# Transposing token tiles and attention outputs by DMA instead of on TensorE

## The chip, the cores and the metric

The kernel runs on one core of one Trainium2 chip. The metric is the device time of one execution in microseconds (us). A result is the median of the timed runs, with the lowest and highest in brackets.

Engines are named as in the profile: PE is TensorE, PEld its weight loads, DVE is VectorE, ACT is ScalarE, SP is SyncE, whose queue issues nearly all DMAs (SPq). Tiles lie in SBUF, the on-chip memory; the results of matmuls go to PSUM, a second one, which is divided into banks.

## The reference

Two layers are run twice with the same weights on 2048 tokens of width 1024 (x + A(norm x), then x + B(norm x)). A is a dilated local attention with 32 heads, window 8 and step 2: token s sees tokens s, s-2, ..., s-14. B is an MLP over the token axis: its first matmul sums over the tokens.

```python
def _A_ref(x, wqkv, wo):
    H = 32; Dh = D // H
    W, dil = 8, 2
    qkv = ((x @ wqkv).reshape(B, S, 3, H, Dh)).transpose(2, 0, 3, 1, 4)
    q, k, v = qkv[0], qkv[1], qkv[2]
    # ... gather of 8 keys and values a token, softmax over them ...
    o = jnp.einsum("bhsw,bhswd->bhsd", attn, vg)
    return o.transpose(0, 2, 1, 3).reshape(B, S, D) @ wo

def _B_ref(x, w1, b1, w2, b2):          # S = 2048, F = 3584
    h = _layernorm(x, axis=-1)
    u = _gelu(jnp.einsum("bsd,sf->bdf", h, w1) + b1)
    y = jnp.einsum("bdf,fs->bds", u, w2) + b2
    return y.transpose(0, 2, 1)

x = A_x
x = x + _A_ref(_layernorm(x), A_wqkv, A_wo)
x = x + _B_ref(_layernorm(x), B_w1, B_b1, B_w2, B_b2)
x = x + _A_ref(_layernorm(x), A_wqkv, A_wo)
x = x + _B_ref(_layernorm(x), B_w1, B_b1, B_w2, B_b2)
```

## The kernel before

Even and odd tokens never meet in attention, so they are two classes of 1024 tokens. A class is worked in four chunks of 8 heads: eight chunks a layer, four of class 0, then four of class 1. In a chunk TensorE makes q, k and v, and VectorE does scores, softmax and the weighted sum.

The kernel's matmuls sum over the partitions, the leading axis of a tile, so two things are transposed on TensorE: the normed tokens, before the q, k, v projections (`hT`), and the attention outputs, before the output projection (`oT`). A transpose on TensorE is a matmul against an identity. It leaves its result in PSUM, and ScalarE (in one case VectorE) copies it to SBUF.

```python
    stat = pool("stat", 4)
    x2p = pool("x2p", 5)
    hxp = pool("hxp", 4)
    pers = pool("pers", 1)
    wqp = pool("wqp", 2)
    wbp = pool("wbp", 6)
    otp = pool("otp", NQ)
    dram = pool("dram", 1, space=bass.MemoryType.DRAM)
    psmm = pool("psmm", 2, space=bass.MemoryType.PSUM)
    pstp = pool("pstp", 1, space=bass.MemoryType.PSUM)
    psop = pool("psop", 2, space=bass.MemoryType.PSUM)
    psgp = pool("psgp", 2, space=bass.MemoryType.PSUM)
# ... cut ...
    def ps_fill(k):
        pl, tag = ((psop, "pso"), (psgp, "psg"))[k % 2]
        return pl.tile([P, 512], FP32, name=tag, tag=tag)
# ... cut ...
    o_q = pers.tile([P, J, QW], BF16, name="o_q")
# ... cut ...
    g = [pers.tile([P, GF, D], BF16, name=f"g{n}") for n in range(NFB)]
# ... cut ...
    def transposes(h, tag="tpf"):
        tp = pstp.tile([P, KD, P], BF16, name="tp", tag=tag)
        for kt in range(KD):
            nc.tensor.transpose(tp[:, kt, :], h[:, kt * P:(kt + 1) * P], ident[:])
        return tp
# ... cut ...
    def prologue_tile(c, j, hT):
        t = g[(c * J + j) // GF][:, (c * J + j) % GF, :]
        if c:
            nm, rs = stats_act(t, 1.0, eps1)
            norm_act(t, t, nm, rs)
        else:
            mean, rs = stats_dve(t, 1.0, eps1)
            norm_dve(t, t, mean, rs)
        tp = transposes(t, "tpf" if c or j % 2 else "tpa")
        nc.scalar.copy(out=hT[c][j // JH][:, :, j % JH, :], in_=tp[:])
```

The kernel uses eight banks of PSUM: two for `ps`, one for each of the two tags of `pstp` (the transposes), two for `pso` and two for `psg`.

```python
                tf = T4[:].rearrange("p u j c -> p u (j c)")
                for n in range(W // WB):
                    self.weighted(ci, n * WB, WB, T4[:])
                    if n == 0:
                        nc.vector.tensor_tensor(out=of, in0=tf[:, 0], in1=tf[:, 1], op=ALU.add)
                        yield 0.0, 3.5
                    else:
                        nc.vector.tensor_tensor(out=tf[:, 0], in0=tf[:, 0], in1=tf[:, 1], op=ALU.add)
                        nc.vector.tensor_tensor(out=of, in0=of, in1=tf[:, 0], op=ALU.add)
                        yield 0.0, 4.8
            oT = otp.tile([P, 2, J, P], BF16, name="oT", tag="oT")
            self.oT[c][qi] = oT
            for b in range(2):
                tp = pstp.tile([P, J, P], BF16, name="tpo", tag="tpa")
                for j in range(J):
                    nc.tensor.transpose(tp[:, j, :], o_q[:, j, b * P:(b + 1) * P], ident[:])
                nc.scalar.copy(out=oT[:, b, :, :], in_=tp[:])
            yield 1.2, 0.0
```

There is one `o_q` buffer. The next chunk may write it only when the transposes of this chunk have read it.

```python
        for n in range(NDC):
            for hf in range(2):
                wt = wb("wo", [P, KD // 2, 512])
                for k in range(KD // 2):
                    kt = hf * (KD // 2) + k
                    nc.sync.dma_start(out=wt[:, k, :], in_=wo_v[kt // 2, kt % 2][:, :, n * 512:(n + 1) * 512])
                wo_t[n][hf] = wt
# ... cut ...
        for j in range(J):
            xr = x2("xr")
            nc.sync.dma_start(out=xr[:], in_=res_v[:, j, :])
            xn = x2("xn")
            s1 = st("s1", [P, NDC]) if on_act else None
            for n in range(NDC):
                ps = psop.tile([P, 512], FP32, name="pso", tag="pso")
                xs_ = slice(n * 512, (n + 1) * 512)
                for kt in range(KD):
                    nc.tensor.matmul(ps[:], lhsT=at_.oT[c][kt // 2][:, kt % 2, j, :], rhs=wo_t[n][kt // 4][:, kt % 4, :],
# ... cut ...
    def gemm1(h2, fb, classes, first, last):
        wt = {c: w1_tile(c, fb) for c in classes}
        nk = len(classes) * J
        for fl in range(GF):
            ft = fb * GF + fl
            for dc in range(NDC):
                ps = ps_both(fl * NDC + dc) if last and first else ps_fill(fl * NDC + dc)
                k = 0
                for c in classes:
                    for j in range(J):
                        nc.tensor.matmul(ps[:], lhsT=wt[c][:, j, fl * P:(fl + 1) * P],
                                         rhs=h2[c][j // JH][:, j % JH, dc * 512:(dc + 1) * 512],
# ... cut ...
    def gemm2_tile(c, i, w2t, src, dst, hT, on_act=False):
        xs = x2("xs")
        nc.sync.dma_start(out=xs[:], in_=src[c][i * P:(i + 1) * P, :])
        xo = x2("xo")
        for dc in range(NDC):
            ps = ps_fill(dc)
            for ft in range(FT):
                nc.tensor.matmul(ps[:], lhsT=w2t[ft // HF][:, ft % HF, c::DIL],
                                 rhs=g[ft // GF][:, ft % GF, dc * 512:(dc + 1) * 512],
                                 start=(ft == 0), stop=(ft == FT - 1))
# ... cut ...
            norm_dve(hb[:], xo[:], mean, rs)
        tp = transposes(hb)
        for jh in range(2):
            src_v = tp[:].rearrange("d kt (a jh j) -> d jh kt j a", jh=2, j=JH)[:, jh]
            dst_v = hT[c][jh][:, :, :, 16 * i:16 * i + 16]
            if on_act or jh == 0:
                nc.scalar.copy(out=dst_v, in_=src_v)
            else:
                nc.vector.tensor_copy(out=dst_v, in_=src_v)
        yield 0.6, 0.0 if on_act else 2.0
```

The sum of class 0's tokens over ten of the fourteen 256-wide blocks of F (320 matmuls, the "partials") needs only class 0's attention. It is issued as filling while VectorE is still busy with class 1. How far ahead it is issued is set by `weave`: each `yield` hands it a pair of numbers, an estimate in us of TensorE's and of VectorE's work, and it puts filling in while TensorE's sum is below VectorE's. Each block has one `w1` tile and four groups of eight matmuls, two in each pool.

```python
def partials():
    for fb in range(NPART):                      # NPART = 10
        yield from gemm1(h2, fb, (0,), True, False)

weave(at_.stream(), second_class(),
      chain(out_proj(at_, 0, res[0], xa[li][0], h2, on_act=True), partials()),   # filling
      out_proj(at_, 1, res[1], xa[li][1], h2, on_act=False))
for fb in range(NPART, NFB):
    run(gemm1(h2, fb, (0, 1), True, True))       # the other four blocks, both classes
for fb in range(NPART):
    run(gemm1(h2, fb, (1,), False, True))        # class 1's half of the ten
```

## Time and profile before

The median before is 1398.31 us (1396.37 to 1399.87, 4 runs). The profiled execution spans 1394.9 us at a granted TensorE clock of 0.983. These lines of the page say how busy the engines are in all, with the number of instructions at the end:

```profile
PE 1314.1 (94%) x7840; PEld 749.7 (54%) x7840; DVE 818.0 (59%) x928; ACT 483.4 (35%) x940; POOL 10.5 (1%) x20
```

94% is an average over stages with different limits, so the same is read by stretches. The table of busy time by stretch has, per row: start and end of the stretch, its length, then busy time and count for PE, PEld, DVE, ACT and POOL, then the granted clock (1.00 is full), the DMA share and GB/s. The stretches are the prologue, attention 1, the MLP of layer 1, the two halves of attention 2 (class 0 with the other class's second MLP matmul as filling; class 1), and the rest.

```profile
0.00:39.00 39.00, 24.02 (x208) 19.23 (x209) 15.74 (x36) 28.78 (x68) 10.49 (x20) 0.98 0.95 246
39.00:359.00 320.00, 300.01 (x2168) 203.85 (x2167) 295.45 (x300) 165.09 (x332) 0.00 (x0) 0.99 0.33 97
359.00:620.00 261.00, 259.73 (x1249) 118.66 (x1248) 88.52 (x144) 57.07 (x100) 0.00 (x0) 0.99 0.44 130
620.00:840.00 220.00, 207.48 (x1482) 140.06 (x1481) 175.32 (x174) 92.34 (x180) 0.00 (x0) 0.98 0.48 140
840.00:1034.00 194.00, 167.77 (x1107) 107.28 (x1104) 164.49 (x156) 90.91 (x182) 0.00 (x0) 0.95 0.34 97
1034.00:1395.00 361.00, 355.09 (x1636) 160.65 (x1636) 78.46 (x121) 49.26 (x79) 0.00 (x0) 0.99 0.34 101
```

Attention 1 belongs to VectorE (295 of 320 us), the two MLP stretches to TensorE (259.7 of 261, 355.1 of 361 us), and attention 2 is mixed. Since the last stretch is dense TensorE work, any matmul that can be done before 1034 us shortens it. That is what the filling is for.

Here is the end of attention 2, from the timeline of PE. A row has start, length, engine, source line, operation, output and inputs, count and, in brackets, idle time before it and what ended it. L466 is `gemm1`, L433 the output projection, L357 the transposes of the attention output.

```profile
1006.13 1.03 PE L466 MATMUL psg<-h_8331,w_9361 128*128 128x512 bf16 x4
1006.99 2.75 PE L433 MATMUL pso<-wo,oT 128*128 128x512 bf16 x12
1009.58 1.03 PE L466 MATMUL psg<-h_8330,w_9721 128*128 128x512 bf16 x4
...
1015.62 1.03 PE L466 MATMUL psg<-h_8331,w_9763 128*128 128x512 bf16 x4
1034.35 1.03 PE L357 MATMUL tpo<-ident,o_q 128*128 128x128 bf16 x8 [17.70 <-DVE o_q L350]
...
1039.99 10.36 PE L433 MATMUL pso<-wo,oT 128*128 128x512 bf16 x37 [0.36 <-DVE xn L439]
```

At 1006.99 us twelve matmuls of the output projection for class 1 start: two accumulations, six of the eight terms of each. Both `pso` banks are taken, and they can't be finished before the last chunk's `oT` exists, which has the other two terms. Then four groups run, all in `psg`, and TensorE stands for 17.70 us until VectorE has made the last `o_q`. The same stretch in the table of windows:

```profile
1016.00:1034.00 18.00, 0.65 (x4) 0.10 (x1) 17.55 (x12) 0.58 (x1) 0.00 (x0) 0.63 0.00 0
1034.00:1045.00 11.00, 8.95 (x33) 3.88 (x34) 4.38 (x9) 2.52 (x4) 0.00 (x0) 0.52 0.16 49
```

TensorE is busy 0.65 of 18 us, its granted clock is 0.63 and then 0.52, and no DMA moves (0 GB/s).

The longest wait of VectorE on the transposes is this line of the list of waits (who waited for what: us in total, times, longest), and the timeline around its end:

```profile
DVE o_q L346 <- PE tpo L357: 23.8, 1, 23.8
```
```profile
940.30 0.99 ACT L358 COPY oT<-tpo 128x1024 bf16<-128x1024 bf16 x1
...
941.34 0.61 PE L357 MATMUL tpo<-ident,o_q 128*128 128x128 bf16 x8
...
941.99 1.22 DVE L346 TENSOR_TENSOR o_q<-T_126 128x2048 bf16<-128x2048 bf16 x1 [23.78 <-PE tpo L357]
```

VectorE wants to write the next `o_q`, and the second half of the previous chunk's transposes has not read the old one. It waits for the copy at 940.30, which comes late in ScalarE's queue behind the norms of the output projection.

In the second MLP matmul, TensorE's timeline shows what one token tile's eight transposes cost:

```profile
604.99 0.38 PE L488 MATMUL pso<-g_138,w_5535 128*128 128x512 bf16 x1
605.52 0.62 PE L228 MATMUL tp<-ident,hb 128*128 128x128 bf16 x8 [0.16 <-DVE hb L218]
605.98 0.38 PE L488 MATMUL pso<-g_138,w_5535 128*128 128x512 bf16 x1
```

The dense stream has a 128x512 matmul every 216 ns; here 0.99 us lie between two of them, so the transposes and the wait before them cost 0.77 us.

### The profile page before, as it was taken

What the parts mean: (1) busy time and instruction counts of PE and PEld (TensorE: products, weight loads), DVE (VectorE), ACT (ScalarE), POOL (GpSimd) and SP (SyncE); (2) the same over time, 40 slices, a digit from 0 to 9 for tenths busy, and PEclk for the clock granted to TensorE, in tenths of its full rate; (3) what the DMA queues carried; (4) which work ended last, traced back from release to release, by engine and by line L of the source; (5) the groups of instructions that cost most, each with busy time, mean ns of one, the idle gap of its engine ahead of it and who ended that gap; (6) DMA issues with size and microseconds to landing.
All of it is one profiled execution on the core that took longest, in us unless ns stands there. A gap on an engine that the chain in (4) does not pass through costs nothing.

```text
span 1394.9 us, 18742 instructions
## 1 busy us (share of the span) xinstructions
PE 1314.1 (94%) x7840; PEld 749.7 (54%) x7840; DVE 818.0 (59%) x928; ACT 483.4 (35%) x940; POOL 10.5 (1%) x20
## 2 busy tenths in 40 slices
PE   6999989999899999999899989899949999999998
PEld 5777656654344444458665458664414444444443
DVE  4869999999820433327999939929976023211111
ACT  7953348633122430013244543475312134100000
POOL 3000000000000000000000000000000000000000
PEclk9999999999999999999999999999969999999999
DMA  9423224532342226653365554334206222243531
GB/s 244 122 72 95 77 66 129 169 94 73 102 136 80 79 72 197 184 156 115 109 172 160 154 162 114 105 102 136 83 16 181 70 81 73 82 137 99 150 99 57
DMA packets 230916, 160.50 MB, mean 115 GB/s; under 512 B 7632, under 2 KB 208336, under 8 KB 230832
## 3 DMA queue, kind: packets, MB, share of 16 engines
q1 hardware_dynamic: 230720, 159.30, 39.3%
q8 instruction: 61, 1.00, 0.3%
q0 software_dynamic: 112, 0.01, 0.1%
q14 instruction: 23, 0.19, 0.0%
HBM read 127.94 MB, written 16.78 MB: 104 GB/s over the span
## 4 chain that ended last, share of the span: by engine, by line
PE 56%; DVE 35%; ACT 6%; issue 2%; DMA 2%; SPq 0%; DVEq 0%; ACTq 0%
PE psg L488 11%; PE pso L488 9%; PE psg L466 9%; DVE T_126 L321 8%; PE ps L273 7%; DVE T_126 L288 7%; PE pso L433 6%; PE pso L466 5%; PE ps L466 4%; DVE T_126 L289 4%; DVE o_q L350 3%; DVE T_126 L349 3%; DVE T_126 L290 2%; DVE St L291 1%; DVE xo L493 1%
## 5 line engine op out<-in xcount | busy, mean ns | idle before, releaser
L433 PE MATMUL pso<-wo,oT 128*128 128x512 bf16 x512 | 121.5, 389 | 0.7 <-DVE xn L439 0.4
L288 DVE TENSOR_TENSOR T_126<-q_116,k_118 128x4096 bf16<-128x4096 bf16 x32 | 73.2, 2289 | 55.5 <-ACT q_116 L275 36.4
L493 DVE SCALAR_TENSOR_TENSOR xo<-psg,b_sb,xs 128x512 bf16<-128x512 f32 x32 | 24.0, 749 | 124.6 <-PE psg L488 124.6
L493 DVE SCALAR_TENSOR_TENSOR xo<-pso,b_sb,xs 128x512 bf16<-128x512 f32 x32 | 24.0, 750 | 103.9 <-PE pso L488 98.6
L433 PEld LDWEIGHTS <-oT 128*128 128x128 bf16 x512 | 50.4, 100 | 62.2 <-issue 7.5
L321 DVE TENSOR_TENSOR T_126<-v_120,Pb 128x4096 bf16<-128x4096 bf16 (+1 forms) x40 | 74.0, 1864 | 11.7 <-PE psg L336 10.8
L289 DVE TENSOR_TENSOR T_126<-T_126 128x2048 bf16<-128x2048 bf16 x64 | 78.1, 1221 | 1.2
L288 DVE TENSOR_TENSOR T_126<-q_117,k_119 128x4096 bf16<-128x4096 bf16 x32 | 73.1, 2284 | 4.1 <-PE psg L336 2.2
L321 DVE TENSOR_TENSOR T_126<-v_121,Pb 128x4096 bf16<-128x4096 bf16 (+1 forms) x40 | 73.8, 1864 | 0.9
L477 DVE TENSOR_TENSOR tmp<-pso,g_132 128x512 f32<-128x512 f32 x4 | 2.8, 692 | 117.0 <-DMA w_10309<-in_B_w_dram 60.7
L273 PE MATMUL ps<-wq,hT_152 128*128 128x256 bf16 x384 | 51.4, 288 | 4.7 <-DMA wq<-in_A_wqkv_dram 2.1
L273 PE MATMUL ps<-wq,hT_6303 128*128 128x256 bf16 x384 | 46.5, 280 | 4.6 <-ACT v_120 L275 4.2
L273 PE MATMUL ps<-wq,hT_4874 128*128 128x256 bf16 x384 | 46.5, 280 | 4.5 <-ACT v_120 L275 4.1
L357 PE MATMUL tpo<-ident,o_q 128*128 128x128 bf16 x256 | 23.9, 235 | 27.9 <-DVE o_q L350 26.2
L358 ACT COPY oT<-tpo 128x1024 bf16<-128x1024 bf16 x32 | 32.3, 1010 | 47.3 <-PE tpo L357 47.3
L273 PE MATMUL ps<-wq,hT_153 128*128 128x256 bf16 x384 | 44.9, 273 | 3.1 <-ACT hT_153 L244 2.5
L273 PEld LDWEIGHTS <-hT_152 128*128 128x128 bf16 x384 | 38.9, 103 | 14.3 <-ACT hT_152 L244 2.9
L273 PE MATMUL ps<-wq,hT_810 128*128 128x256 bf16 x384 | 44.9, 273 | 1.7 <-ACT q_117 L275 1.0
L273 PE MATMUL ps<-wq,hT_811 128*128 128x256 bf16 x384 | 45.5, 273 | 0.4 <-ACT v_120 L275 0.4
L290 DVE TENSOR_TENSOR T_126<-T_126 128x1024 bf16<-128x1024 bf16 x64 | 44.0, 688 | 1.4
L350 DVE TENSOR_TENSOR o_q<-o_q,T_126 128x2048 bf16<-128x2048 bf16 x36 | 44.1, 1225 | 1.2
L349 DVE TENSOR_TENSOR T_126<-T_126 128x2048 bf16<-128x2048 bf16 x36 | 44.1, 1224 | 1.1
(1405 smaller groups left out, 2629.3 us busy)
## 6 DMA issues: line engine op xcount, KB each, us to landing
wq<-in_A_wqkv_dram SPq DMA_DIRECT2D x48, 512.0 KB, 4.2
wo<-in_A_wo_dram SPq DMA_DIRECT2D x64, 128.0 KB, 2.7
xr<-in_A_x_dram SPq DMA_DIRECT2D x16, 256.0 KB, 3.1
out_dram<-xo SPq DMA_DIRECT2D x16, 256.0 KB, 2.2
k_118<-k_118 SPq DMA_DIRECT2D x8, 392.0 KB, 5.0
v_120<-v_120 SPq DMA_DIRECT2D x8, 392.0 KB, 5.0
k_119<-k_119 SPq DMA_DIRECT2D x8, 392.0 KB, 5.0
v_121<-v_121 SPq DMA_DIRECT2D x8, 392.0 KB, 4.9
```

The costliest lines, as they stand in the source:

```text
L273: nc.tensor.matmul(ps[:, jj, :], lhsT=self.hT[c][j // JH][:, kt, j % JH, :], rhs=wts[part][:, kt, :], start=(kt == 0), stop=(kt == KD - 1))
L288: nc.vector.tensor_tensor(out=flat, in0=qb, in1=windows(k, u0, WB, [(1, J * QW)]), op=ALU.mult)
L289: nc.vector.tensor_tensor(out=pr[:, :, 0:16, :], in0=pr[:, :, 0:16, :], in1=pr[:, :, 16:32, :], op=ALU.add)
L290: nc.vector.tensor_tensor(out=pr[:, :, 0:8, :], in0=pr[:, :, 0:8, :], in1=pr[:, :, 8:16, :], op=ALU.add)
L321: nc.vector.tensor_tensor(out=dst.rearrange("p u j (d h) -> p u j d h", h=HQ), in0=v, in1=pw, op=ALU.mult)
L349: nc.vector.tensor_tensor(out=tf[:, 0], in0=tf[:, 0], in1=tf[:, 1], op=ALU.add)
L350: nc.vector.tensor_tensor(out=of, in0=of, in1=tf[:, 0], op=ALU.add)
L358: nc.scalar.copy(out=oT[:, b, :, :], in_=tp[:])
L433: nc.tensor.matmul(ps[:], lhsT=at_.oT[c][kt // 2][:, kt % 2, j, :], rhs=wo_t[n][kt // 4][:, kt % 4, :], start=(kt == 0), stop=(kt == KD - ...
L466: nc.tensor.matmul(ps[:], lhsT=wt[c][:, j, fl * P:(fl + 1) * P], rhs=h2[c][j // JH][:, j % JH, dc * 512:(dc + 1) * 512], start=(k == 0), s ...
L488: nc.tensor.matmul(ps[:], lhsT=w2t[ft // HF][:, ft % HF, c::DIL], rhs=g[ft // GF][:, ft % GF, dc * 512:(dc + 1) * 512], start=(ft == 0), s ...
L493: nc.vector.scalar_tensor_tensor(out=xo[:, dc * 512:(dc + 1) * 512], in0=ps[:], scalar=b2_sb[:, i, c:c + 1], in1=xs[:, dc * 512:(dc + 1) * ...
```

## The change

The intent is to take all transposes off TensorE. The transposing DMA reads SBUF and writes SBUF, so the PSUM banks of the transposes and the copies by ScalarE go too. The two banks are given to the accumulators (`pso` and `psg` have three each). In layer 2 the copies had scattered a tile of 128 consecutive tokens to slots; the DMA writes the tile as it stands, so `hT` is kept in token order and the projection reads its weights with a step of eight tokens. With the transposes two estimates for `weave` go as well, the 1.2 us of a chunk and the 0.6 us of a tile of the second MLP matmul.

```diff
-    pstp = pool("pstp", 1, space=bass.MemoryType.PSUM)
-    psop = pool("psop", 2, space=bass.MemoryType.PSUM)
-    psgp = pool("psgp", 2, space=bass.MemoryType.PSUM)
+    psop = pool("psop", 3, space=bass.MemoryType.PSUM)
+    psgp = pool("psgp", 3, space=bass.MemoryType.PSUM)
 # ... cut: def transposes(h, tag) removed ...
-        tp = transposes(t, "tpf" if c or j % 2 else "tpa")
-        nc.scalar.copy(out=hT[c][j // JH][:, :, j % JH, :], in_=tp[:])
+        nc.sync.dma_start_transpose(out=hT[c][:, j, :, :], in_=t)
+    def new_hT(hT, c, by_slot):
+        hT[c] = hx(f"hT{c}", [P, J, KD, P] if by_slot else [P, KD, SC])
+        def lhs(self, c, kt, j):
+            return self.hT[c][:, j, kt, :] if self.first else self.hT[c][:, kt, j::J]
 # ... cut: proj takes lhsT=self.lhs(c, kt, j) ...
-            oT = otp.tile([P, 2, J, P], BF16, name="oT", tag="oT")
+            oT = otp.tile([P, J, 2, P], BF16, name="oT", tag="oT")
             self.oT[c][qi] = oT
-            for b in range(2):
-                tp = pstp.tile([P, J, P], BF16, name="tpo", tag="tpa")
-                for j in range(J):
-                    nc.tensor.transpose(tp[:, j, :], o_q[:, j, b * P:(b + 1) * P], ident[:])
-                nc.scalar.copy(out=oT[:, b, :, :], in_=tp[:])
-            yield 1.2, 0.0
+            nc.sync.dma_start_transpose(out=oT[:].rearrange("p j b q -> p (j b) q"), in_=of)
 # ... cut: out_proj reads oT[:, j, kt % 2, :]; h2 becomes one tile ...
-        tp = transposes(hb)
-        for jh in range(2):
-            src_v = tp[:].rearrange("d kt (a jh j) -> d jh kt j a", jh=2, j=JH)[:, jh]
-            dst_v = hT[c][jh][:, :, :, 16 * i:16 * i + 16]
-            # ... cut: copied by ScalarE or VectorE ...
-        yield 0.6, 0.0 if on_act else 2.0
+        nc.sync.dma_start_transpose(out=hT[c][:, :, i * P:(i + 1) * P], in_=hb[:])
+        yield 0.0, 0.0 if on_act else 2.0
```

More of the change, by code (lines that the diff above doesn't have):

```diff
@@ L53 @@
     NSLOT = J + W - 1
-    JH = J // 2
     SC = S // DIL
@@ L73 @@
     x2p = pool("x2p", 5)
-    hxp = pool("hxp", 4)
+    hxp = pool("hxp", 2)
     pers = pool("pers", 1)
@@ L223, in norm_act @@
         nc.scalar.activation(out=dst, in_=x, func=ACT.Identity, bias=bi[:], scale=rs[:])
-    def transposes(h, tag="tpf"):
-        tp = pstp.tile([P, KD, P], BF16, name="tp", tag=tag)
-        for kt in range(KD):
-            nc.tensor.transpose(tp[:, kt, :], h[:, kt * P:(kt + 1) * P], ident[:])
-        return tp
     def x_stage(c, j):
@@ L242, in prologue_tile @@
             norm_dve(t, t, mean, rs)
-        tp = transposes(t, "tpf" if c or j % 2 else "tpa")
-        nc.scalar.copy(out=hT[c][j // JH][:, :, j % JH, :], in_=tp[:])
-    def new_hT(hT, c):
-        for jh in range(2):
-            hT[c][jh] = hx(f"hT{c}{jh}", [P, KD, JH, P])
+        nc.sync.dma_start_transpose(out=hT[c][:, j, :, :], in_=t)
+    def new_hT(hT, c, by_slot):
+        hT[c] = hx(f"hT{c}", [P, J, KD, P] if by_slot else [P, KD, SC])
     chunks = [(c, qi) for c in range(DIL) for qi in range(NQ)]
@@ L272, in proj @@
                         for kt in range(KD):
-                            nc.tensor.matmul(ps[:, jj, :], lhsT=self.hT[c][j // JH][:, kt, j % JH, :], rhs=wts[part][:, kt, :],
+                            nc.tensor.matmul(ps[:, jj, :], lhsT=self.lhs(c, kt, j), rhs=wts[part][:, kt, :],
                                              start=(kt == 0), stop=(kt == KD - 1))
@@ L421, in out_proj @@
                 wo_t[n][hf] = wt
-        for jh in range(2):
-            h2[c][jh] = hx(f"h2{c}{jh}", [P, JH, D])
+        h2[c] = hx(f"h2{c}", [P, J, D])
         for j in range(J):
@@ L432, in out_proj @@
                 for kt in range(KD):
-                    nc.tensor.matmul(ps[:], lhsT=at_.oT[c][kt // 2][:, kt % 2, j, :], rhs=wo_t[n][kt // 4][:, kt % 4, :],
+                    nc.tensor.matmul(ps[:], lhsT=at_.oT[c][kt // 2][:, j, kt % 2, :], rhs=wo_t[n][kt // 4][:, kt % 4, :],
                                      start=(kt == 0), stop=(kt == KD - 1 and not on_act))
@@ L440, in out_proj @@
             nc.sync.dma_start(out=dst_v[:, j, :], in_=xn[:])
-            h = h2[c][j // JH][:, j % JH, :]
+            h = h2[c][:, j, :]
             if on_act:
@@ L466, in gemm1 @@
                         nc.tensor.matmul(ps[:], lhsT=wt[c][:, j, fl * P:(fl + 1) * P],
-                                         rhs=h2[c][j // JH][:, j % JH, dc * 512:(dc + 1) * 512],
+                                         rhs=h2[c][:, j, dc * 512:(dc + 1) * 512],
                                          start=(k == 0), stop=(k == nk - 1))
@@ L505, in gemm2_tile @@
             norm_dve(hb[:], xo[:], mean, rs)
-        tp = transposes(hb)
-        for jh in range(2):
-            src_v = tp[:].rearrange("d kt (a jh j) -> d jh kt j a", jh=2, j=JH)[:, jh]
-            dst_v = hT[c][jh][:, :, :, 16 * i:16 * i + 16]
-            if on_act or jh == 0:
-                nc.scalar.copy(out=dst_v, in_=src_v)
-            else:
-                nc.vector.tensor_copy(out=dst_v, in_=src_v)
-        yield 0.6, 0.0 if on_act else 2.0
+        nc.sync.dma_start_transpose(out=hT[c][:, :, i * P:(i + 1) * P], in_=hb[:])
+        yield 0.0, 0.0 if on_act else 2.0
     def w2_tiles(i):
@@ L552, in weave @@
         run(fill)
-    hT = [[None, None] for _ in range(DIL)]
-    new_hT(hT, 0)
+    hT = [None] * DIL
+    new_hT(hT, 0, True)
     for li in range(2):
@@ L558 @@
         at_ = Attn(hT, (0, 1, 2, 3) if first else (), first)
-        h2 = [[None, None] for _ in range(DIL)]
+        h2 = [None] * DIL
         res = [xin_v[c] for c in range(DIL)] if first else [slots(xb[c]) for c in range(DIL)]
         def second_class():
-            new_hT(hT, 1)
+            new_hT(hT, 1, first)
             for i in range(NT):
@@ L584 @@
                 ln_exp_table()
-            hT = [[None, None] for _ in range(DIL)]
-            new_hT(hT, 0)
+            hT = [None] * DIL
+            new_hT(hT, 0, False)
             for i in range(NT):
```

## The prediction

> **What bounds it now.** No engine alone. The table by stretches, with matmul counts, gives TensorE's real load, because dense streams show 109 ns per 128x256 matmul and 216 ns per 128x512 one: about 1300 of 1395 us. Stages, from the chain of waits and the windows: prologue to 39 us (DMA share 0.95, ScalarE); attention 1, 39 to 359 us, VectorE (295 of 320 us busy); 359 to 620 us TensorE; attention 2, 620 to 1040 us, mixed; 1040 us to the end, pure TensorE, untouched.
>
> **Removed.** 512 TensorE transposes. In the second MLP matmul (525 to 620 us) a token tile's eight cost 0.77 us of stream (timeline, 604.99 to 605.98 us): 8 x 0.77 = 6 us, fully critical. Eight more tiles in attention 2 (6 us) and 16 chunks at 1 to 2 us of TensorE are largely hidden by VectorE. ScalarE loses 32 oT copies of 1.01 us and about 25 us of hT copies, critical only in the prologue. Two PSUM banks join the accumulators; evacuation waits are small, 1 to 3 us.
>
> The largest prize is a wait: at 918 to 942 us VectorE stood 23.8 us (longest entry "DVE o_q from PE tpo") until the second half of oT's transposes had read o_q; these stood behind a ScalarE copy queued behind the output projection. After it VectorE sets the pace, and TensorE then idles about 18 us at 1016 to 1034 us. With a DMA reading o_q this should mostly go: 10 to 18 us.
>
> **Added.** 32 transposing DMAs of 256 KB and 16 of 512 KB on the Sync queue. No transposing DMA is in this trace; plain ones of 256 to 512 KB land in 2 to 5 us. Estimate: 4 to 7 us for 256 KB, 6 to 10 us for 512 KB, against 2 to 3 us by TensorE and ScalarE. Exposed where nothing fills: the last oT of both attentions (359, 1034 us), about +5 us each; hT before the projections at 620 and 825 us, +3 to 4 us each; prologue +3 us, its DMA being full. The queue is in order, so a transpose waiting for VectorE can hold weight loads.
>
> **Moved.** In layer 2 the projection weights are read with a step of eight bf16 (16 bytes): 1536 loads. The Trainium skill, "SBUF — State Buffer", section "Door 1: The DMA port swizzle", says that lines are 16 bytes and that at least two hits per line are needed for full rate; here each load element has its own line. This trace shows only step two costing nothing (98 ns, like dense). The load must stay within the 109 ns of its matmul. I give 45% to an excess of 15 to 60 ns (estimate): +23 to 90 us of TensorE, two thirds exposed.
>
> **Sum.** -6 -6 -14 +10 +7 +3 = -6 us: about 1392 without the stride, which adds 15 to 60 us in 45% of cases. Predicted 1400 us, 1370 to 1470. Faster by over 2%: 0.12; within 2%: 0.58; slower by over 2%: 0.30.
>
> **What would show it.** Spacing of layer 2's 128x256 matmuls (109 ns before) and their load times (98 ns); second-MLP tiles shrinking from 12.87 to 12.1 us at 525 to 620 us; the 23.8 us o_q wait gone; longer idle before the first output-projection matmul after each attention; issue-to-landing of transposes within 4 to 10 us; the final stage of 197 us unchanged.
>
> **What would make it wrong.** Strided loads at 200 ns (over +100 us, slower); transposes that take 15 us or more, or block the Sync queue, stretching tails, the prologue and w2 loads; an order in which the o_q-freeing DMA stands behind stores waiting for ScalarE, so that the 23.8 us wait stays; or, upward, freed PSUM and ScalarE shortening attention 2 by 30 us or more.

## More of the kernel before

The six buffers of `wbp` hold the weights of the output projection, of the first MLP matmul and of the second one.

The output projection accumulates in `pso` alone. The first MLP matmul, `gemm1`, alternates its groups between `pso` and `psg`.

## The result and the profile after

After: 1375.03 us (1372.74 to 1379.47, 4 runs) against 1398.31 us. The ratio is 0.9838 (95% interval 0.9809 to 0.9867), so the change is 1.6% faster. A ratio is the mean time of one kernel's fast runs over that of the other's of the same rounds, so it is not quite the ratio of the medians that are quoted.

The profiled execution after spans 1371.0 us at a granted clock of 0.985; it was the fastest of the four runs, and a part of TensorE's matmul records is missing from it (7226 matmuls where the loads number 7328). So busy times of PE after are a few us too low, and counts of matmuls too.

```profile
PE 1276.0 (93%) x7226; PEld 741.0 (54%) x7328; DVE 811.1 (59%) x920; ACT 426.2 (31%) x868; POOL 10.5 (1%) x20
```

Rows of the same table for the stages that moved most, with bounds at the same events (prologue, the two halves of attention 2, the rest):

```profile
0.00:43.00 43.00, 18.45 (x136) 14.86 (x137) 15.88 (x36) 21.47 (x59) 10.50 (x20) 0.97 1.01 228
...
619.00:836.00 217.00, 199.72 (x1335) 143.95 (x1348) 174.52 (x173) 76.98 (x158) 0.00 (x0) 0.97 0.63 159
836.00:1026.00 190.00, 177.81 (x1111) 118.34 (x1123) 164.90 (x156) 86.37 (x178) 0.00 (x0) 0.99 0.41 112
1026.00:1371.00 345.00, 334.78 (x1519) 151.94 (x1550) 77.40 (x121) 45.00 (x73) 0.00 (x0) 0.99 0.36 105
```

With the bounds taken to a tenth of a microsecond, the difference of 23.9 us is made up so:

| stage | before, us | after, us | difference |
|---|---|---|---|
| start to the first score of VectorE | 39.5 | 43.1 | +3.6 |
| attention 1 | 318.9 | 319.0 | +0.1 |
| rest of layer 1, to the first projection of layer 2 | 261.3 | 256.6 | -4.7 |
| attention 2, class 0 | 205.1 | 201.4 | -3.7 |
| attention 2, class 1 (to the last `o_q`) | 209.5 | 206.0 | -3.5 |
| to the end | 360.6 | 344.9 | -15.7 |

Two thirds of the gain lie after the last transpose, in a stage in which the change touches nothing but the way that the last `oT` comes. So work must have moved out of that stage. PE's timeline of the end of attention 2 (L454 is `gemm1`, L421 the output projection), the DMA that makes the last `oT`, and the windows:

```profile
1010.46 4.05 PE L421 MATMUL pso<-wo,oT 128*128 128x512 bf16 x18
1014.34 1.89 PE L454 MATMUL psg<-h_7662,w_8846 128*128 128x512 bf16 x8
...
1021.25 1.89 PE L454 MATMUL ps<-h_7662,w_9186 128*128 128x512 bf16 x8
1030.55 15.74 PE L421 MATMUL pso<-wo,oT 128*128 128x512 bf16 x64 [7.41 <-DMA oT<-o_q]
```
```profile
1026.17 1.80 SPq L348 DMA_TRANSPOSE oT<-o_q  x1
```
```profile
1008.00:1026.00 18.00, 15.08 (x70) 6.62 (x68) 17.62 (x12) 1.76 (x3) 0.00 (x0) 1.00 0.16 45
1026.00:1037.00 11.00, 6.45 (x23) 2.63 (x24) 5.11 (x11) 0.50 (x2) 0.00 (x0) 0.69 0.65 171
```

In the 18 us before the end of attention TensorE is now busy 15.08 us at full clock. Before the end of attention 2, at least 344 `gemm1` matmuls are done instead of 288. The last `oT` needs 1026.17 to 1030.55, 4.4 us; before, the two transposes and copies took from 1034.35 to 1038.60, 4.3 us, so nothing is lost there.

VectorE's long wait has hardly changed, only its releaser; the Sync queue's timeline shows why:

```profile
DVE o_q L340 <- DMA oT<-o_q: 20.5, 1, 20.5
```
```profile
923.81 0.41 SPq L414 DMA_DIRECT2D xr<-xb_147  x1
925.31 0.64 SPq L441 DMA_DIRECT2D w_8510<-in_B_w_dram  x1
926.61 3.65 SPq L348 DMA_TRANSPOSE oT<-o_q  x1
```

That chunk's `o_q` was complete at 887.5 us, but its transposing DMA was issued at 926.61. The queue is in order, and ahead of it stood loads of residuals (`xr`), stores of results (`xa`), copies of k and v and loads of weights, each issued only when its own buffer or data was ready.

The second MLP matmul of layer 1 in the chain of waits (start, length, piece), and the loads with a step of eight (the page on one tile: duration in ns as minimum, median and maximum, and the DMA's time to landing):

```profile
514.20 6.04 PE pso L476 x28
...
526.29 6.04 PE pso L476 x28
```
```profile
L267 PEld LDWEIGHTS <-hT_4570 x768: 140/143/169, 618.7 to 737.6; 128*128 128x128 bf16 x192
L267 PE MATMUL ps<-wq,hT_4570 x768: 270/273/421, 618.7 to 737.7; 128*128 128x256 bf16 x192
...
DMA to landing us min/median/max: 4.3/4.5/5.4
```

Tiles follow each other every 12.09 us instead of 12.87. The strided load takes 143 ns (median; the mean is 144) instead of 98, while consecutive 128x256 matmuls in a dense stretch of layer 2 still start 109 ns apart.

### The profile page after: what moved, and what is told of

Same layout as the page of the kernel before. It is cut to its first block, busy times and chain, and to the rows that moved or that the text cites. A ratio compares the mean times of both kernels' runs of the same rounds, so it can differ in the third digit from the quotient of the medians.

```text
span 1371.0 us, 17626 instructions
## 1 busy us (share of the span) xinstructions
PE 1276.0 (93%) x7226; PEld 741.0 (54%) x7328; DVE 811.1 (59%) x920; ACT 426.2 (31%) x868; POOL 10.5 (1%) x20
## 4 chain that ended last, share of the span: by engine, by line
PE 51%; DVE 34%; ACT 6%; DMA 6%; issue 2%; SPq 1%; ACTq 0%; DVEq 0%
PE psg L476 12%; PE pso L476 12%; PE psg L454 8%; DVE T_123 L282 7%; DVE T_123 L315 7%; PE ps L267 6%; PE pso L454 5%; DVE T_123 L283 4%; PE ps L454 3%; PE pso L421 3%; DVE T_123 L343 3%; DVE o_q L344 2%; DVE T_123 L284 2%; DMA oT<-o_q 1%; DVE St L285 1%
## 5 line engine op out<-in xcount | busy, mean ns | idle before, releaser
L421 PE MATMUL pso<-wo,oT 128*128 128x512 bf16 x496 | 120.0, 390 | 24.6 <-DMA oT<-o_q 23.4
L267 PE MATMUL ps<-wq,hT_149 128*128 128x256 bf16 x768 | 93.1, 282 | 28.9 <-DMA wq<-in_A_wqkv_dram 26.3
L267 PEld LDWEIGHTS <-hT_149 128*128 128x128 bf16 x768 | 77.6, 101 | 44.8 <-issue 11.1
L421 PEld LDWEIGHTS <-oT 128*128 128x128 bf16 x512 | 50.6, 100 | 89.1 <-DMA oT<-o_q 25.1
L267 PE MATMUL ps<-wq,hT_5899 128*128 128x256 bf16 x768 | 89.1, 277 | 6.4 <-ACT v_118 L269 3.3
L267 PE MATMUL ps<-wq,hT_4570 128*128 128x256 bf16 x768 | 88.2, 278 | 6.8 <-ACT v_117 L269 4.1
L481 DVE SCALAR_TENSOR_TENSOR xo<-pso,b_sb,xs 128x512 bf16<-128x512 f32 x32 | 23.9, 747 | 116.9 <-PE pso L476 90.2
L267 PEld LDWEIGHTS <-hT_5899 128*128 128x128 bf16 x768 | 86.1, 144 | 11.7 <-issue 7.7
L267 PEld LDWEIGHTS <-hT_4570 128*128 128x128 bf16 x768 | 85.9, 144 | 10.2 <-issue 4.9
L267 PE MATMUL ps<-wq,hT_734 128*128 128x256 bf16 x768 | 87.9, 273 | 3.5 <-ACT v_118 L269 2.1
L267 PEld LDWEIGHTS <-hT_734 128*128 128x128 bf16 x768 | 75.1, 98 | 16.9 <-issue 4.3
L181 ACT ACTIVATE ln<-mv,eps_105 128x1 f32<-128x1 f32 x16 | 4.7, 294 | 104.3 <-DVE mv L190 104.3
```

The costliest lines, as they stand in the source:

```text
L267: nc.tensor.matmul(ps[:, jj, :], lhsT=self.lhs(c, kt, j), rhs=wts[part][:, kt, :], start=(kt == 0), stop=(kt == KD - 1))
L421: nc.tensor.matmul(ps[:], lhsT=at_.oT[c][kt // 2][:, j, kt % 2, :], rhs=wo_t[n][kt // 4][:, kt % 4, :], start=(kt == 0), stop=(kt == KD - ...
L481: nc.vector.scalar_tensor_tensor(out=xo[:, dc * 512:(dc + 1) * 512], in0=ps[:], scalar=b2_sb[:, i, c:c + 1], in1=xs[:, dc * 512:(dc + 1) * ...
```

## The experiments

Twelve kernels ran, each four times in its rounds with the kernel before. All gave correct results except the one that was meant not to. "Filling" below is the number of `gemm1` matmuls done before attention 2 ends, counted in the trace.

The theories, as they stood after reading the traces:

- **BANKS**: the two PSUM banks per accumulator pool that the change frees let the filling run on.
- **LOCK**: the output projection takes the `pso` banks and half of the filling is blocked behind it; the change escapes since its filling is further ahead at that moment or needs those banks less.
- **QUEUE**: the transposes of the last chunk stand in TensorE's in-order queue, waiting for VectorE, with filling behind them; a DMA doesn't stand there.

### The change with two and two banks

```diff
-    psop = pool("psop", 3, space=bass.MemoryType.PSUM)
-    psgp = pool("psgp", 3, space=bass.MemoryType.PSUM)
+    psop = pool("psop", 2, space=bass.MemoryType.PSUM)
+    psgp = pool("psgp", 2, space=bass.MemoryType.PSUM)
```

> The change whole, but the two accumulator pools go back from 3+3 PSUM banks to 2+2 (two banks lie unused). Theory BANKS (the gain of about 13 us at the end of attention 2, where 64 more matmuls of the first MLP product ran before the attention ended, comes from the third banks): 1385 to 1392 us, and TensorE idle for 10 us or more in the last 18 us of attention 2. Theory QUEUE (it comes from transposes no longer standing in TensorE's in-order queue before work that was ready): 1372 to 1379 us, TensorE busy there as in the change.

Measured: 1380.47 us (1379.06 to 1383.91), ratio 0.9873 (0.9851 to 0.9894), filling 352. The median lies in neither range. Some 18 of the 23 us stay without the banks. The 5 us between this median and that of the change may be what the banks are worth, but the two were not timed in the same rounds and their intervals overlap.

### The kernel before with a third bank for the output projection

All TensorE transposes share one bank, and `pso` gets the other.

```diff
-    psop = pool("psop", 2, space=bass.MemoryType.PSUM)
+    psop = pool("psop", 3, space=bass.MemoryType.PSUM)
-        tp = transposes(t, "tpf" if c or j % 2 else "tpa")
+        tp = transposes(t)
-                tp = pstp.tile([P, J, P], BF16, name="tpo", tag="tpa")
+                tp = pstp.tile([P, J, P], BF16, name="tpo", tag="tpf")
```

> The kernel before with its TensorE transposes; the two banks for transposes are merged into one and the freed bank goes to the output-projection pool (3+2). BANKS: TensorE runs on in the last 18 us of attention 2, 1383 to 1391 us. QUEUE: no gain, 1394 to 1405 us, TensorE idle there for 15 us or more as before.

Measured: 1397.92 us (1396.27 to 1399.53), ratio 0.9994 (0.9974 to 1.0014), filling 288. PE's timeline of this kernel:

```profile
1009.58 4.05 PE L433 MATMUL pso<-wo,oT 128*128 128x512 bf16 x18
1013.46 7.22 PE L466 MATMUL psg<-h,w 128*128 128x512 bf16 x32
1037.15 1.03 PE L357 MATMUL tpo<-ident,o_q 128*128 128x128 bf16 x8 [16.47 <-DVE o_q L350]
```

The output projection took three banks (18 matmuls, six of eight terms in each) where it had taken two. Again only `psg` groups follow, and TensorE stands 16.47 us. A bank more is a bank more for the holder of the lock. BANKS, as the cause of the main gain, is refuted.

### Attention outputs alone by DMA

The `oT` part of the change in the kernel before; normed tokens stay on TensorE, PSUM as before.

```diff
+            oT = otp.tile([P, J, 2, P], BF16, name="oT", tag="oT")
+            nc.sync.dma_start_transpose(out=oT[:].rearrange("p j b q -> p (j b) q"), in_=of)
 # ... the loop of transposes and copies goes, out_proj reads oT[:, j, kt % 2, :] ...
```

> Only the attention outputs are transposed by DMA; normed tokens by TensorE as before, PSUM 2+2 as before. QUEUE: most of the gain at the end of attention 2 is here, 1379 to 1387 us. BANKS: 1392 to 1399 us, the end of attention 2 as before. Both: the layer-2 projection weights stay dense (98 ns loads).

Measured: 1383.38 us (1382.62 to 1386.07), ratio 0.9893 (0.9874 to 0.9913), filling 344. The wait for `o_q` is 23.3 us. The time is in the range of QUEUE; the next run tests it further.

### Normed tokens alone by DMA

The change with the `oT` loop of the kernel before put back, `pstp` with its one bank, and two banks for each accumulator pool.

```diff
+    pstp = pool("pstp", 1, space=bass.MemoryType.PSUM)
-            nc.sync.dma_start_transpose(out=oT[:].rearrange("p j b q -> p (j b) q"), in_=of)
+            for b in range(2):
+                tp = pstp.tile([P, J, P], BF16, name="tpo", tag="tpa")
+                for j in range(J):
+                    nc.tensor.transpose(tp[:, j, :], o_q[:, j, b * P:(b + 1) * P], ident[:])
+                nc.scalar.copy(out=oT[:, b, :, :], in_=tp[:])
```

> Only normed tokens are transposed by DMA; attention outputs by TensorE as before, PSUM 2+2 as before. Both theories: the second MLP's tiles shrink from 12.87 to 12.1 us (-6 us), some more in attention 2 (0 to -6), the prologue loses 3 to 4 us: 1386 to 1397 us; end of attention 2 idle as before (15 us or more). Layer-2 weight loads 144 ns.

Measured: 1387.73 us (1383.72 to 1390.01), ratio 0.9911 (0.9886 to 0.9937), filling 336. PE's timeline:

```profile
1016.55 2.75 PE L427 MATMUL pso<-wo,oT 128*128 128x512 bf16 x12
...
1030.34 1.89 PE L460 MATMUL ps<-h,w 128*128 128x512 bf16 x8
1038.47 1.03 PE L352 MATMUL tpo<-ident,o_q 128*128 128x128 bf16 x8 [6.24 <-DVE o_q L345]
```

The time is in the expected range, but the idle time of 15 us or more that both theories expected is not there. The last chunk's transposes still stand in TensorE's queue, and TensorE still stands before them, but only 6.24 us: the filling got its turn first. QUEUE in its strict form is refuted. The two halves gain 15.1 and 10.7 us, together more than the whole (18 us with the same banks). Both remove the same idle time, so their gains don't add.

What the kernels share is how much of the filling was done when the output projection of class 1 took its banks:

| kernel | `gemm1` matmuls before that | left of 320 | filling in all |
|---|---|---|---|
| before | 256 | 64 | 288 |
| before, third bank | 256 | 64 | 288 |
| normed tokens alone | 280 | 40 | 336 |
| attention outputs alone | 296 | 24 | 344 |
| the change, two and two banks | 312 | 8 | 352 |

352 is all that can run before class 1's tokens are there: 320 and, of the next blocks, four groups' first eight matmuls. The 344 of the attention outputs alone is a full count, since its trace has all 7584 matmuls; the 344 seen in the change itself is short of 352 by missing records.

With 64 left, two whole blocks are open, their `pso` halves can't run, and both `w1` tiles stay in use. With the four weight tiles of the output projection these are all six buffers of `wbp`; the last load of a `w1` tile before the idle time is issued at 1007.18 us, and in the window of 1016 to 1034 us nothing moved by DMA (0 GB/s, shown above). With 40 or fewer left, only one block or none is open, a next `w1` tile can be loaded, and the first 32 matmuls of the next blocks run, which use `psg` and `ps`. That the six buffers are the second half of the lock is read from the code and these counts; no run changed their number.

What sets the counts at that point was not tested by a run, but the code shows it: the estimates for `weave`. The kernels were rebuilt for this, without a chip. First, TensorE's order is fixed in the program: in the 13 kernels whose traces miss no matmul the output tiles of TensorE's matmuls come in the order of the trace. So the lock works when the program is laid out, and on the chip TensorE follows that order. Second, with all transposes left on TensorE and only the estimates set to 0, the kernel before gets 280 (without the 0.6 us), 296 (without the 1.2 us) or 312 (without both) of these matmuls before the output projection, and 336, 344 or 339 before the last chunk's transposes. With both estimates put back, the change gets 256 and 288 as the kernel before. The head start of the filling thus comes from the estimates that were deleted together with the transposes, not from the time that the transposes took. No run timed the estimates alone.

### The kernel before, filling in the other pool alone

One line makes the partial sums use `psg` only, so that they never meet the output projection. All transposes stay on TensorE.

```diff
-                ps = ps_both(fl * NDC + dc) if last and first else ps_fill(fl * NDC + dc)
+                ps = ps_both(fl * NDC + dc) if last and first else ps_fill(fl * NDC + dc if last else 1)
```

> The kernel before, all transposes on TensorE; only the accumulators of the first MLP product's early half (the work that fills attention 2) always come from the psg pool instead of taking turns between pso and psg. Theory LOCK (at the end of attention 2 this work is ready but stands behind banks of pso that output-projection groups hold while they wait for the last attention output): 32 to 64 more of these matmuls run before attention 2 ends (288 before), 7 to 14 us: 1384 to 1391 us. Theory QUEUE (the transposes in TensorE's queue are what blocks it): 288 as before, 1394 to 1402 us.

Measured: 1383.42 us (1382.68 to 1385.12), ratio 0.9893 (0.9876 to 0.991), filling 344. PE's timeline and the window of the former idle time:

```profile
1010.82 2.75 PE L433 MATMUL pso<-wo,oT 128*128 128x512 bf16 x12
1013.41 15.70 PE L466 MATMUL psg<-h,w 128*128 128x512 bf16 x72
...
1034.73 1.01 PE L357 MATMUL tpo<-ident,o_q 128*128 128x128 bf16 x8 [2.16 <-DVE o_q L350]
```
```profile
1016.00:1034.00 18.00, 16.56 (x77) 7.35 (x75) 17.55 (x12) 4.09 (x7) 0.00 (x0) 1.00 0.20 59
```

The output projection still takes both `pso` banks, at 1010.82 with the same 256 matmuls done. But 72 matmuls follow in `psg`, TensorE is busy 16.56 of 18 us at full clock, and the idle time before the transposes is 2.16 us. The time is just below the range of LOCK. This one line gives 15.6 us by the medians, about as much as the last stage gave in the change (15.7). LOCK is shown as the cause in the kernel before.

### The change with the same line

> The change, with the filling work's accumulators from psg alone. If the change already removed the lock by itself (344 of these matmuls ran before the end of attention 2): nothing more to win, 1371 to 1378 us. If the change's gain is another one and the two add: 1358 to 1366 us.

The edit is the line above. Measured: 1375.93 us (1374.51 to 1381.89), ratio 0.9844 (0.9816 to 0.9872), filling 352. It gives nothing on top of the change. The change and the line remove the same idle time.

### A second buffer for the attention output, in the change

A second `o_q` doesn't fit in SBUF (it lacks some 3 KB a partition), but the last tile of `g` is free during attention, so two chunks of each layer put their output there.

```diff
-            of = o_q[:].rearrange("p j c -> p (j c)")
+            of = (g[NFB - 1] if ci in (5, 7) else o_q)[:].rearrange("p j c -> p (j c)")
```

> The change, but the second and fourth quarter of heads of the second token class write the attention output into a tile that lies idle then, so that VectorE doesn't wait for the DMA that reads o_q. If the 20.5 us wait is on the critical path: attention 2 ends 12 to 20 us earlier and the time falls by 5 to 14 us, 1361 to 1370 us. If TensorE's own work sets the pace there: 1372 to 1378 us, and TensorE's idle time moves elsewhere.

Measured: 1365.8 us (1362.86 to 1368.73), ratio 0.9756 (0.9733 to 0.9779), faster. The wait is gone, and attention 2 ends at 1012.9 us, with filling 307. So the wait was on the critical path, and the change had left it there.

### A second buffer in the kernel before

> The kernel before, all transposes on TensorE; only the second and fourth quarter of heads of the second token class get an attention-output buffer of their own, as in the run of the changed kernel that did so. If the o_q wait (23.8 us here) is a cost of the buffer and not of how it is transposed: it goes, and the time falls by 5 to 14 us, 1384 to 1393 us. If TensorE's in-order transposes make the gain impossible: 1394 us or more.

The edit is the same, with the TensorE transposes reading `of`. Measured: 1380.9 us (1377.45 to 1384.8), ratio 0.9863 (0.9842 to 0.9883), filling 256. That is better than the expected range: the buffer alone gives about 18 us with all transposes on TensorE.

### Both repairs in the kernel before

The second buffer and the filling in `psg`, all transposes on TensorE.

> The kernel before, all transposes on TensorE, with both repairs: the filling work's accumulators from psg alone (1383.4 us alone) and the second attention-output buffer (1380.9 us alone). If the change won by unlocking the filling work and nothing of it is owed to the transposing DMAs themselves: as fast as the changed kernel with the second buffer, 1363 to 1369 us. If taking 512 transposes off TensorE is worth something once lock and wait are gone (they cost some 30 us of its queue): 1371 to 1379 us.

Measured: 1381.41 us (1379.23 to 1385.05), ratio 0.987 (0.9847 to 0.9894), filling 245, slower than both ranges. The repairs don't add. With the second buffer attention ends at 1016.5 us, and the output projection comes when the filling, begun at 952.3, has done only 256 matmuls: the lock no longer matters, but how far the filling has come does. In the change with the second buffer the filling begins at 939.1 us, and 307 are done at 1012.9. The kernels differ by 15.6 us in their medians (not of the same rounds); 62 more matmuls at 216 ns are 13.4 us of that. This does not show a gain owed to the transposes' own time: the kernel here keeps the estimates of 1.2 and 0.6 us. Rebuilt without them, its transposes still on TensorE, it too has 312 of the matmuls before the output projection, as many as the change with the second buffer; it was not timed.

### Dense weights in layer 2, with a wrong result

```diff
-            return self.hT[c][:, j, kt, :] if self.first else self.hT[c][:, kt, j::J]
+            return self.hT[c][:, j, kt, :] if self.first else self.hT[c][:, kt, SC - P:SC]
```

> The change, but every layer-2 projection reads the 128 dense weight columns of the last token tile instead of every eighth column; the result is wrong on purpose. If the 16-byte step costs time (loads of 144 ns against 98 ns, within a matmul spacing of 109 ns): loads back to 98 ns and 8 to 25 us faster than the change, 1350 to 1367 us. If the load stays hidden: loads back to 98 ns and 1370 to 1378 us.

Measured: 1375.18 us (1374.34 to 1381.52), ratio 0.984 (0.9815 to 0.9865); the relative error is 1.15, as meant. The page on the source line:

```profile
L267 PEld LDWEIGHTS <-hT x3072: 95/98/152, 10.9 to 961.9; 128*128 128x128 bf16 x192
```

The loads are back at 98 ns and the time has not moved. The step of eight costs 45 ns a load, and nothing of it shows, since the loads overlap the stream.

### Projection weights loaded ahead of the transposes

The first matmul of the change waits for weights whose load stands behind transposing DMAs in the Sync queue. Here the two loads are issued before them.

```diff
-                both = self.proj(0, 1, 0)
+                both = self.proj(0, 1, 0, wts=self.load(0, 1, 0))
 # ... load() is the part of proj that allocates wq and starts its DMA ...
```

> The change, with the first two projection weights loaded before the first transposes in program order. If the 3.6 us that the prologue lost come from these loads standing behind the transposes in the Sync queue: the first matmul before 14 us (18.1 in the change), attention starts at 38 to 41 us (43.1) and 1370 to 1373 us. If they come from the transposes themselves: attention still starts at 42 us or later, 1374 to 1377 us.

Measured: 1377.91 us (1375.56 to 1379.32), ratio 0.9848 (0.983 to 0.9865). The first matmul starts at 21.9 us, later than in the change (18.1), and now waits for `hT`; attention starts at 47.0 us. The stretch of 10 to 20 us, in the windows of the kernel before, of the change, and of this kernel (share and GB/s last):

```profile
10.00:20.00 10.00, 7.50 (x52) 5.66 (x53) 8.19 (x22) 7.57 (x20) 1.06 (x2) 1.00 1.20 236
```
```profile
10.00:20.00 10.00, 1.93 (x10) 1.45 (x11) 8.19 (x20) 2.28 (x9) 1.07 (x2) 1.00 1.11 157
```
```profile
10.00:20.00 10.00, 0.00 (x0) 0.00 (x0) 8.64 (x21) 2.48 (x10) 1.05 (x2) 1.00 1.44 95
```

With the DMA engines just as full (shares of 1.20, 1.11 and 1.44; packets overlap) they move 236, 157 and 95 GB/s. So it was not the order in the queue: in these windows transposing DMAs beside full plain traffic moved less in all. Why they did is not shown.

### The mixture

The change with the second buffer, and with the tokens of layer 1's prologue transposed by TensorE into a `psg` bank.

```diff
-        nc.sync.dma_start_transpose(out=hT[c][:, j, :, :], in_=t)
+        tp = psgp.tile([P, KD, P], BF16, name="tp", tag="psg")
+        for kt in range(KD):
+            nc.tensor.transpose(tp[:, kt, :], t[:, kt * P:(kt + 1) * P], ident[:])
+        nc.scalar.copy(out=hT[c][:, j, :, :], in_=tp[:])
```

> The changed kernel with the second attention-output buffer, and the layer-1 normed tokens transposed by TensorE again (into a psg bank that lies idle then). If the prologue's loss is transposing DMAs beside a full DMA queue: first projection matmul at 11 to 13 us instead of 18, attention starts at 39 to 41 us, 1359 to 1363 us. If it is not: attention starts at 42 us or later and 1364 to 1368 us.

Measured: 1362.65 us (1362.0 to 1367.09), ratio 0.9747 (0.9727 to 0.9767), faster, and the best of all. The first matmul starts at 11.7 us as before the change, the first score at 40.9. Against the change with the second buffer alone the 3 us are of the size that the prologue had lost, but the two ran in different rounds and their ranges overlap, so this last step is suggested, not shown.

## Why the prediction was right or wrong

The range (1370 to 1470) and the class (within 2%) held. The centre, 1400, was 25 us too high, and the change was not neutral but faster. That the range held was in part luck: of the 14 us for the wait 3 came, the 17 us of tails were too high, and two thirds of the gain came through work that the sum doesn't have.

- **What bounds it**: right. The final stage of 197 us is unchanged (1197.4 to 1394.9 before, 1173.5 to 1371.0 after), and the stages have the limits that were named.
- **Second MLP matmul, -6 us**: right. Tiles shrank from 12.87 to 12.09 us. The stage gained 4.7 us, since its end waits 4.84 us for the last transposing DMA. The 8 tiles in attention 2 stood at another 6 us; that stretch gained 3.7.
- **The wait for `o_q`, -14 us**: wrong, and in the way that the prediction names as what would make it wrong. 20.5 of 23.8 us stayed, since the transposing DMA stood behind waiting loads and stores in the in-order Sync queue. That the wait is on the critical path was right: the second buffer, which removes it, gave 9 us in the change and 18 in the kernel before.
- **Tails, +10 us for the last `oT`, +7 us for `hT`**: too high. 512 KB landed in 4.4 us, not the 6 to 10 of the estimate, and the path by TensorE and ScalarE had taken 4.3 us, not 2 to 3. For `oT` the term is about zero.
- **Prologue, +3 us**: right, 3.6.
- **The step of eight**: the risk of 45% did not come. The Trainium skill, "SBUF — State Buffer", section "Door 1: The DMA port swizzle (why `[64,N]` ≈ `[32,N]`)", asks for two hits per 16-byte line, and the load did become slower, 98 to 143 ns. But matmuls still followed each other every 109 ns, and dense loads made the kernel no faster. The prediction's test, that the load "must stay within the 109 ns of its matmul", was wrong: a load of 143 ns did not slow the stream. This risk had lifted the centre from 1392 to 1400.
- **The step that failed**: the sum has no term for the filling. The prediction calls the stretch from 1040 us on "pure TensorE, untouched". It saw TensorE's idle 18 us at 1016 to 1034 us and ascribed them to VectorE's pace alone, while `gemm1` work was there that could have filled them and was locked out. The experiments show what stood in its place: with 64 of 320 partial matmuls open when the output projection takes both `pso` banks, the filling stops; with 40 or fewer it goes on. The change came to that point with few left, since its edit also deleted the estimates that pace the filling; the prediction doesn't speak of them. It gained 64 matmuls (288 against 352, of which its trace shows 344), 13.8 us at 216 ns, of the 15.7 us of the last stage. The rest was not tested apart; TensorE's clock may have a part in it: in the last 18 us of attention and the 11 us after it the granted clock was 0.63 and 0.52 before, and 1.00 and 0.69 after. The Trainium skill, "TensorE: Matmul & The Clock Gate", section "Part 1: The HAM clock gate (the "warmup" mystery)", says that idle time of more than about 3.4 us halves the clock; this trace agrees in kind.

What remains open: how much of its gain the change would keep with the estimates for `weave` put back, and how much the kernel before would gain by their deletion alone. Neither was timed, so a gain of the transposing DMAs themselves is shown for the second MLP matmul (12.87 to 12.09 us a tile) but not for the end of attention 2. The filling also begins 8 to 10 us earlier, counted from the start of class 1, with both kinds of transposes gone (by 2.7 us with either); in the rebuilt programs its start moves with the same estimates. How much of the 5 us between two and three banks is real is open too. A profile is a single execution; attention 1, whose code is the same in the change and in the kernel with dense weights, ended at 362.1 us in one profile and at 367.5 in the other, so terms of a few us in the table of stages are uncertain.

## What to carry to other kernels

When work is moved off an engine and the time falls, look first at what else the edit changed. Here two numbers that pace the filling went with the work, and most of the gain was in idle time that one line about accumulator banks removes just as well. Filling must not share a pool with a consumer that takes its buffers early and then waits; and a buffer whose release was held up by an in-order queue (here by a transposing DMA that waits in it) was mended by a second buffer, not by another way to transpose. Gains that remove the same idle time don't add, so measure each repair alone, both, and both in the other version before calling one the cause; and where estimates in the code decide the order of work, hold them fixed in one run.

## What the Trainium skill lacked or had wrong

- "SBUF — State Buffer", "Door 1: The DMA port swizzle": for weight loads the page gives no cost of a step. A step of 16 bytes made a 128x128 load 143 ns instead of 98, and it stayed hidden under a stream of one 128x256 matmul every 109 ns.
- "Advanced Engine Details and Errata", section "X-Bar Transpose (TRN2)", says that transpose DMAs are as fast as regular DMAs. Issued when no DMA had moved for 5 us, a 512 KB transpose landed in 4.4 us, where plain 512 KB weight loads took a median of 4.7 us in the same kernel, which agrees as far as it goes. Beside full plain traffic it did not hold: in the prologue throughput fell from 236 to 157 GB/s, and to 95 with weight loads put in front. No page says what a mixture costs.
- "VectorE: DVE Perf Modes", section "The three transpose paths", gives 1309 ns for one 128x128 block by DMA and 390 ns on TensorE. In a stream both are far less: sixteen blocks landed in 4.4 us, 0.27 us each, and eight transposes on TensorE took 0.46 us of its stream (605.52 to 605.98), 57 ns each. The table names PSUM as the destination but has no time for the copy out of it: here, with that copy, both paths took 4.3 to 4.4 us from end to end.
- No page says what a transposing DMA in an in-order queue can wait for: here 39 us passed between the last write of its source (887.5 us) and its issue (926.61 us), while VectorE waited 20.5 us for the buffer.
